# Zero-tile matmuls in PE's planned waits: two layers of memory attention and gated FFN

## The chip, the core and the metric

The kernel runs on one core of one Trainium2 chip. The metric is the device time of one execution in microseconds (us), as the median of several runs. Engines are named as in the profile: PE is TensorE (PEld its weight loads), DVE VectorE, ACT ScalarE, POOL GpSimd, SP SyncE, which here only issues DMAs.

## The reference

Inputs are bf16. `A` is attention over segments of 32 tokens with 8 memory tokens carried from one segment to the next; `B` is a gated feed-forward. The same weights are used twice.

```python
# x: 1 x 2048 x 512; 32 heads of 128; memory 8, segment 32; F = 1792
def A(x, mem0):                       # x is layer-normed
    mem = mem0
    for s in range(64):
        h = concat([mem, x[:, 32*s:32*s+32]])            # 40 tokens
        q, k, v = h @ Wq, h @ Wk, h @ Wv                 # 32 heads
        p = softmax(where(mask, q @ k.T * scale, -1e9))
        o = (p @ v) @ Wo                                 # summed over heads
        mem = o[:, :8]; outs.append(o[:, 8:])
    return concat(outs)
def B(x): return (sigmoid(x @ w_gate) * (x @ w_up)) @ w_down

x = x + A(layernorm(x)); x = x + B(layernorm(x))
x = x + A(layernorm(x)); x = x + B(layernorm(x))
```

## The kernel before

The 64 segments must follow one another, since each takes its memory from the one before. The second layer's attention starts 6 steps behind the first (`lag=6`), so there are 70 steps; in steps 6 to 63 both layers' segments are worked on together (`both`, 80 columns), and at the beginning and the end one alone (40 columns). `emit_step` writes one step: for groups of six heads, the q and k projections (L734, 40 or 80 columns streamed past 128x128 weights), their eviction by ACT into `qku`, the scores (L748), mask, max, exp, sum and product on DVE and ACT (L762 to L780) into `pb`, a transpose on PE (L791) and its copies into `ptsb`, the product with v (L814), an eviction into `otsb`, and the output projection (L832), which accumulates all heads into one bank `WB`. The memory columns of `WB` are copied into the next step's `hT` by DVE (L845, L850). The v rows of the memory come from `strips` (L660, four 32-row outputs beside each other), those of the tokens from `v_pass` (L583, 512 columns), which go to a DRAM scratch `scr` and are read back into `vsb` by DMA (L703). `layernorm_T` transposes a normalised block of 128 tokens (L552); `ffn` runs a block of 128 tokens through the gated feed-forward (L900 transposes, L932 gate and up, L956 down), with weights streamed by POOL.

At the beginning, in the boot, SP issues all attention weights in pieces (L484), and `v_group` runs `v_pass` for many blocks whose results are staged in the FFN's weight tiles and stored to `scr`.

The order of work is not written by hand. Each piece is a `Task` with an engine, a planned duration and its reads and writes. `Planner.plan` runs a list scheduler over all tasks with these planned times, 24 rounds, and keeps the shortest; it also assigns buffers, among them the eight PSUM banks (`bank`). `run` then emits the tasks in the order of their planned starts, and each engine keeps that order. Semaphore waits are put in from the tiles that are read and written. The planned start of a task, `tk.start`, and the planned duration, `tk.dur`, are still there when the instructions are emitted. A matmul of n columns is planned with `max(n / 2.4 + 2.3, 26.0)` ns.

Of the kernel before, what the change touches and what calls it, by code (L numbers as in the profile page):

```python
# [2 lines left out]

# [6 lines left out]
BF16 = mybir.dt.bfloat16  # L10
# [6 lines left out]
P = 128  # L17
# [14 lines left out]
def mm_ns(n):  # L32
    return max(n / 2.4 + 2.3, 26.0)
# [13 lines left out]


class Task:
    __slots__ = ("eng", "dur", "lat", "fn", "deps", "succ", "tail", "boost", "ndep", "ready", "start", "idx", "on", "fresh", "acq", "rel", "durs", "tick", "prev", "land", "adj", "banks")  # L50

    def __init__(self, eng, dur, lat, fn, boost):
        self.durs = dur if isinstance(dur, dict) else {e: dur for e in eng}
        self.eng, self.dur, self.lat, self.fn, self.boost = eng, min(self.durs.values()), lat, fn, boost
        self.deps, self.succ, self.fresh = set(), [], set()
        self.acq, self.rel = [], []
        self.on = None
        self.land = 3000.0
        self.adj = {}
        self.banks = ()  # L60


class Buf:

    __slots__ = ("pool", "kind", "users", "first", "left", "slot", "t_free", "t_prev", "rd")
# [16 lines left out]
class Planner:  # L82
# [3 lines left out]
    LAT = {"PE": 205.0, "DVE": 110.0, "ACT": 128.0, "POOL": 40.0, "SP": 4000.0}  # L86
    TO_PE = 32.0
    WAIT = 65.0

    def __init__(self):  # L90
        self.tasks = []
        self.writer = {}
        self.readers = {}
        self.bufs = []
# [6 lines left out]
    def add(self, eng, dur, fn, r=(), w=(), lat=None, boost=0.0, use=(), late=0.0):  # L101
        engs = eng if isinstance(eng, tuple) else (eng,)
        tk = Task(engs, dur, self.LAT[engs[0]] if lat is None else lat, fn, boost)
        tk.idx = len(self.tasks)
        for k in r:
            if k in self.writer:
                tk.deps.add(self.writer[k])
                tk.fresh.add(self.writer[k])
        for k in w:
            if k in self.writer:  # L110
                tk.deps.add(self.writer[k])
            for q in self.readers.get(k, ()):
                tk.deps.add(q)
        for k in w:
            self.writer[k] = tk.idx
            self.readers[k] = []
        for k in r:
            self.readers.setdefault(k, []).append(tk.idx)
        tk.deps.discard(tk.idx)
        if late:  # L120
            tk.adj = {d: late for d in tk.fresh if self.tasks[d].eng == ("PE",)}
        self.tasks.append(tk)
        if engs[0] != "PE":
            tk.banks = tuple(k for k in r if isinstance(k, Buf) and k.pool.psum)
        for k in list(r) + list(w) + list(use):
            if isinstance(k, Buf) and (not k.users or k.users[-1] != tk.idx):
                k.users.append(tk.idx)
        return tk
# [78 lines left out]
    def forward(self):  # L207
# [126 lines left out]
        order.sort(key=lambda k: (k.start, k.idx))  # L334
        return order

    def waits(self, tk, seen):

        T = self.tasks
        need = {}  # L340
        for d in [T[i] for i in list(tk.deps) + tk.prev]:
            k = d.on if d.on != "SP" else ("SP", d.tick)
            if d.tick > seen.get(k, 0):
                need[k] = max(need.get(k, 0), d.tick)
        seen.update(need)
        return len(need)
# [10 lines left out]
class Kern:  # L357
# [40 lines left out]
    def setup_tiles(self):  # L398
        ctx, tc, nc = self.ctx, self.tc, self.nc
        D, DC, H, HG, F, FC, R = self.D, self.DC, self.H, self.HG, self.F, self.FC, self.R  # L400
        HE = H * P
        c = ctx.enter_context(tc.tile_pool(name="c", bufs=1))
        dr = ctx.enter_context(tc.tile_pool(name="dr", bufs=1, space=bass.MemoryType.DRAM))
        self.scr = [dr.tile([self.NSEG * XS, HE], BF16, name=f"scr{j}") for j in range(2)]
        self.wq = c.tile([P, DC, HE], BF16, name="wq_sb")
        self.wk = c.tile([P, DC, HE], BF16, name="wk_sb")
        self.wv = c.tile([P, DC, HE], BF16, name="wv_sb")
        self.wo = c.tile([P, H, D], BF16, name="wo_sb")
        cst = c.tile([P, P + 2 * L + 8], BF16, name="cst")
        self.ident, self.maskb, self.mask1 = cst[:, 0:P], cst[:, P:P + L], cst[0:L, P + L:P + 2 * L]  # L410
        self.negh = cst[:, P + 2 * L:P + 2 * L + 2].bitcast(F32)
        small = c.tile([P, 48], F32, name="small")
        self.lns = [small[:, 10 * i:10 * i + 10] for i in range(3)]
        self.mx = [small[:, 30 + 6 * i:36 + 6 * i] for i in range(3)]
        self.NV = 3
        self.hT = [c.tile([P, DC, 2 * L], BF16, name=f"hT{i}") for i in range(R)]
        self.qku = [c.tile([P, 3, 2, LW], BF16, name=f"qku{i}") for i in range(3)]
        self.vsb = [c.tile([P, 2, 1024], BF16, name=f"vsb{i}") for i in range(self.NV)]
        self.st = [c.tile([P, HG, L], F32, name=f"st{i}") for i in range(3)]
        self.pb = [c.tile([LW, HG, 64], BF16, name=f"pb{i}") for i in range(3)]  # L420
        self.ptsb = [c.tile([P, HG, 2, L], BF16, name=f"ptsb{i}") for i in range(3)]
        self.otsb = [c.tile([P, HG, 2 * L], BF16, name=f"otsb{i}") for i in range(2)]
        self.NX = 6
        self.xs = [c.tile([P, D], BF16, name=f"xs{i}") for i in range(self.NX)]
        self.xa = [c.tile([P, D], BF16, name=f"xa{i}") for i in range(2)]
        self.oxT = [[c.tile([P, DC, P], BF16, name=f"oxT{j}_{i}") for i in range(2)] for j in range(2)]
        self.xn = [c.tile([P, D], BF16, name=f"xn{i}") for i in range(2)]
        self.xnT = [c.tile([P, DC, P], BF16, name=f"xnT{i}") for i in range(1)]
        self.hff = [c.tile([P, FC, P], BF16, name=f"hff{i}") for i in range(1)]
        self.th = [c.tile([P, 2, P], F32, name=f"th{i}") for i in range(2)]  # L430
        self.xvf = [c.tile([P, DC, P], BF16, name=f"xvf{i}") for i in range(2)]
        self.xvl = [c.tile([P, DC, P], BF16, name=f"xvl{i}") for i in range(3)]
        self.vst = [c.tile([P, 512], BF16, name=f"vst{i}") for i in range(3)]
        self.sst = [c.tile([P, 2, 512], BF16, name=f"sst{i}") for i in range(1)]
        self.NG, self.ND = 3, 3
        self.wg = [c.tile([P, DC, 2 * P], BF16, name=f"wg{i}") for i in range(self.NG)]
        self.wu = [c.tile([P, DC, 2 * P], BF16, name=f"wu{i}") for i in range(self.NG)]
        self.wd = [c.tile([P, 2, D], BF16, name=f"wd{i}") for i in range(self.ND)]
        pp = ctx.enter_context(tc.tile_pool(name="ps", bufs=1, space=PSUM))
        self.bank = Pool([pp.tile([P, 512], F32, name=f"bank{i}") for i in range(8)], {"bg": 3, "v": 3}, psum=True)  # L440
        self.qkp = Pool(self.qku)
        self.vstp = Pool(self.vst)
        self.sstp = Pool(self.sst)
        self.bootp = Pool([fview(w[:, 0, 0:1], [(1, 1024)]) for w in self.wd + self.wg + self.wu])
        self.xnp = Pool(self.xn)

    def setup_consts(self):
        nc, tc = self.nc, self.tc
        cmasks.make_identity(nc, self.ident[:])
        NEG = -1.0e9 / self.scale  # L450
        nc.gpsimd.memset(self.maskb[:], 0.0)
        nc.gpsimd.memset(self.mask1[:], 0.0)
        nc.gpsimd.affine_select(out=self.mask1[:], in_=self.mask1[:], pattern=[[-1, L]],
                                compare_op=ALU.is_ge, fill=NEG, base=0, channel_multiplier=1)
        nc.gpsimd.memset(self.mask1[0:MEM, :], 0.0)
        nc.gpsimd.affine_select(out=self.maskb[0:L, 0:SEG], in_=self.maskb[0:L, 0:SEG], pattern=[[-1, SEG]],
                                compare_op=ALU.is_ge, fill=NEG, base=0, channel_multiplier=1)
        nc.vector.memset(self.negh[:], -0.5)

    def clear(self):  # L460
# [208 lines left out]
    def emit_step(self, t):  # L669
# [10 lines left out]
        nj = len(jobs)  # L680
        full = slice(0, LW)
        hkeys = [("hT", slot, j, k) for j in jobs for k in ("m", "x")]

        c0 = 0 if both else L * j0

# [166 lines left out]
        for idx, j in enumerate(jobs):  # L852
# [3 lines left out]
            dst = self.oxT[j][oi][:, :, (s % BLK) * SEG:(s % BLK + 1) * SEG]  # L856
            pl.add("ACT", 160, lambda dst=dst, a=48 * j - c0: (dst, wo3(a, SEG)), r=[WB], w=[("oxT", j, oi, s % BLK)])

    def last_weights(self):

        if self.lw is None:
# [163 lines left out]
    def run(self):  # L1025
# [3 lines left out]
        order = self.pl.plan()  # L1029
        with self.tc.manual_schedule():  # L1030
            self.setup_consts()
            for tk in order:
                got = tk.fn()
                if isinstance(got, tuple) and len(got) == 3:
                    {"SP": nc.sync, "POOL": nc.gpsimd}[tk.on].dma_start(out=got[1], in_=got[2])
# [63 lines left out]
```

## Time and profile before

| | |
|---|---|
| median of 9 runs | 1827.17 us (1823.74 to 1830.45) |
| the profiled execution | 1825.57 us |
| its span, first to last instruction | 1823.8 us |
| mean granted PE clock over the span | 0.995 |
| PE busy | 1761.5 us, 97% |
| DVE, ACT, POOL busy | 1177.6, 1175.6, 580.2 us |
| longest groups | L734 622.4 and 621.4 us, L832 367.1 us, L932 172.2 and 171.6 us |
| DMA | 271.18 MB, mean 149 GB/s; 341 GB/s in the first of 40 slices |
| PE's longest sums of waits | otsb from ACT before L832 9.1 us (31 times), xn from DVE before L552 7.6 us (5 times) |

A line of a group or of the timeline gives the start, the busy time, engine, line, operation, tiles written and read, the shape and the number of instructions, and in brackets the engine's idle time just before with what ended it. A row of the table of windows gives the stretch, its length, busy time and number of instructions of each engine, the granted PE clock (1.00 is full), the share of the DMA engines' time and the GB/s moved. Matmul records overlap, because matmuls are pipelined: the distance of the starts is the time that one takes.

### The profile page before, as it was taken

How to read it: one execution, taken by the hardware profiler on the slowest of the kernel's cores; microseconds unless marked ns; L12 is line 12 of the kernel's file. 1: busy time of each engine (PE TensorE's matmuls, PEld its weight loads, DVE VectorE, ACT ScalarE, POOL GpSimd, SP SyncE). 2: the span in 40 equal slices, each digit the busy share in tenths (PEclk: the TensorE clock that was granted, in tenths of full speed). 3: DMA queues.
4: the chain of work that ended last, by engine and by line, in shares of the span. 5: the costliest groups of instructions: out<-in, count | busy, mean ns of one | idle time of the engine just before them, and what ended most of it. 6: DMA issues, size and time to landing. Idle time of an engine off the chain costs nothing.

```text
span 1823.8 us, 91963 instructions
## 1 busy us (share of the span) xinstructions
PE 1761.5 (97%) x39743; PEld 1521.7 (83%) x39942; DVE 1177.6 (65%) x3933; ACT 1175.6 (64%) x2969; POOL 580.2 (32%) x838
## 2 busy tenths in 40 slices
PE   7999999999999999999999999999999999999998
PEld 3677787988888898988888898888888898889886
DVE  4466565676676567666666667666766676566665
ACT  5666666676666666665666666666666666566664
POOL 7223031413333242423324142323324231332422
PEclk9999999999999999999999999999999999999999
DMA  9734252636555464645446463555546453554543
GB/s 341 242 108 141 55 149 82 196 104 176 143 153 162 115 182 113 173 126 171 144 129 188 112 184 108 153 151 149 163 115 189 128 158 107 167 147 117 174 126 109
DMA packets 137096, 271.18 MB, mean 149 GB/s; under 512 B 32698, under 2 KB 69186, under 8 KB 136690
## 3 DMA queue, kind: packets, MB, share of 16 engines
q0 software_dynamic: 56736, 183.35, 34.1%
q1 hardware_dynamic: 79954, 81.94, 15.7%
q8 instruction: 313, 5.13, 1.2%
q14 instruction: 93, 0.76, 0.1%
HBM read 220.93 MB, written 26.21 MB: 136 GB/s over the span
## 4 chain that ended last, share of the span: by engine, by line
PE 86%; ACT 5%; SPq 3%; DVE 3%; issue 2%; DMA 1%; POOL 0%; ACTq 0%; POOLq 0%; DVEq 0%
PE bank L734 32%; PE bank L832 17%; PE bank L932 9%; PE bank L660 7%; PE bank L583 6%; PE bank L956 4%; PE bank L748 4%; PE bank L814 3%; SPq L484 3%; PE bank L791 2%; ACT qku L1039 1%; ACT ptsb L1039 1%; ACT otsb L1039 1%; PE bank L552 1%; DVE st L762 1%
## 5 line engine op out<-in xcount | busy, mean ns | idle before, releaser
L734 PE MATMUL bank<-hT,wq_sb 128*128 128x80 bf16 (+1 forms) x8960 | 622.4, 198 | 8.7 <-issue 4.6
L734 PE MATMUL bank<-hT,wk_sb 128*128 128x80 bf16 (+1 forms) x8960 | 621.4, 198 | 2.8 <-DMA wk_sb<-in_A_Wk_dram 2.7
L1039 ACT CAST qku<-bank 128x480 bf16<-128x480 f32 (+3 forms) x770 | 391.4, 512 | 253.8 <-PE bank L734 184.4
L734 PEld LDWEIGHTS <-wq_sb 128*128 128x128 bf16 x8960 | 454.7, 99 | 38.3 <-issue 27.5
L734 PEld LDWEIGHTS <-wk_sb 128*128 128x128 bf16 x8960 | 450.4, 99 | 4.2 <-DMA wk_sb<-in_A_Wk_dram 3.2
L762 DVE TENSOR_TENSOR st<-bank,cst 40x240 f32<-40x240 f32 (+3 forms) x768 | 279.1, 367 | 227.0 <-PE bank L748 219.4
L832 PE MATMUL bank<-otsb,wo_sb 128*128 128x80 bf16 (+1 forms) x8960 | 367.1, 198 | 10.8 <-ACT otsb L1039 9.1
L924 POOL DMA_DIRECT2D wg<-in_B_w_gate_dram x217 | 164.8, 760 | 647.5 <-PE bank L932 623.7
L832 PEld LDWEIGHTS <-wo_sb 128*128 128x128 bf16 x8960 | 342.0, 99 | 24.0 <-issue 15.1
L1039 ACT CAST otsb<-bank 128x480 bf16<-128x480 f32 (+3 forms) x420 | 196.3, 486 | 72.5 <-PE bank L814 53.7
L950 POOL DMA_DIRECT2D wd<-in_B_w_down_dram x217 | 153.5, 710 | 154.7 <-PE bank L791 71.9
L1039 ACT COPY ptsb<-bank 40x240 bf16<-40x240 bf16 (+2 forms) x552 | 173.9, 316 | 38.7 <-PE bank L791 30.4
L772 ACT ACTIVATE st<-st 80x240 f32<-80x240 f32 (+3 forms) x420 | 159.4, 382 | 37.0 <-DVE st L769 32.8
L774 DVE TENSOR_REDUCE small<-st 80x6 f32<-80x240 f32 (+3 forms) x420 | 151.7, 364 | 47.0 <-ACT st L772 44.1
L932 PE MATMUL bank<-xnT,wg 128*128 128x128 bf16 (+2 forms) x1784 | 172.2, 219 | 1.1 <-ACT xnT L1039 0.5
L932 PE MATMUL bank<-xnT,wu 128*128 128x128 bf16 (+2 forms) x1784 | 171.6, 219 | 0.0
L925 POOL DMA_DIRECT2D wu<-in_B_w_up_dram x217 | 162.8, 750 | 3.2 <-issue 2.5
L769 DVE TENSOR_TENSOR st<-st,small 80x240 f32<-80x240 f32 (+3 forms) x420 | 154.0, 369 | 4.0
L767 DVE TENSOR_REDUCE small<-st 80x6 f32<-80x240 f32 (+3 forms) x420 | 152.6, 365 | 5.5
L779 DVE TENSOR_TENSOR pb<-st,small 80x240 bf16<-80x240 f32 (+3 forms) x420 | 152.5, 369 | 4.5
L748 PE MATMUL bank<-qku 128*128 128x80 bf16 (+1 forms) x2240 | 154.1, 198 | 1.1 <-ACT qku L1039 0.2
L542 POOL TENSOR_TENSOR small<-small,cst 128x1 f32<-128x1 f32 (+1 forms) x80 | 44.5, 557 | 346.4 <-DVE small L541 343.9
(93 smaller groups left out, 2248.7 us busy)
## 6 DMA issues: line engine op xcount, KB each, us to landing
wg<-in_B_w_gate_dram POOLq DMA_DIRECT2D x220, 256.0 KB, 4.1
wu<-in_B_w_up_dram POOLq DMA_DIRECT2D x220, 256.0 KB, 4.7
wd<-in_B_w_down_dram POOLq DMA_DIRECT2D x220, 256.0 KB, 4.8
vsb<-scr SPq DMA_DIRECT2D x476, 48.0 KB
vsb<-sst SPq DMA_DIRECT2D x480, 32.0 KB
scr<-vst SPq DMA_DIRECT2D x120, 96.0 KB
wq_sb<-in_A_Wq_dram SPq DMA_DIRECT2D x10, 384.0 KB
wk_sb<-in_A_Wk_dram SPq DMA_DIRECT2D x10, 384.0 KB
```

The costliest lines, as they stand in the source:

```text
L734: nc.tensor.matmul(o_ap, lhsT=W[:, c, h * P:(h + 1) * P], rhs=mv(c), start=(c == 0), stop=(c == DC - 1))
L748: nc.tensor.matmul(s_all(SB)[:, w0 + i, :], lhsT=fview(qku[:, i, 0, 0:1], [(1, P)]), rhs=qku[:, i, 1, 0:ncol], start=True, stop=True)
L762: pl.add("DVE", dve_ns(n, True), lambda gsz=gsz, hs=hs, st=st, SB=SB, pj_=pj_, npj_=npj_, mk=mk, idx=idx: nc.vector.tensor_tensor(out=st[p ...
L767: pl.add("DVE", dve_ns(n), lambda hs=hs, st=st, mx=mx: nc.vector.tensor_reduce(out=mx[pr, hs], in_=st[pr, hs], axis=AX.X, op=ALU.max), r=s ...
L769: pl.add("DVE", dve_ns(n), lambda gsz=gsz, hs=hs, st=st, mx=mx: nc.vector.tensor_tensor(out=st[pr, hs], in0=st[pr, hs], in1=mx[pr, hs].uns ...
L772: pl.add("ACT", act_ns(n), lambda hs=hs, st=st: nc.scalar.activation(out=st[pr, hs], in_=st[pr, hs], func=ACTF.Exp, scale=self.scale), r=s ...
L832: nc.tensor.matmul(WB[:, c * ncol:(c + 1) * ncol], lhsT=self.wo[:, h, c * P:(c + 1) * P], rhs=otsb[:, hl, 0:ncol], start=(h == 0 and c == ...
L924: pl.add("POOL", 760, lambda wg=wg, fs=fs: nc.gpsimd.dma_start(out=wg[:], in_=self.wgv[:, :, fs]), r=[("wo", self.H - 1)], w=[gk] + bt, la ...
L925: pl.add("POOL", 760, lambda wu=wu, fs=fs: nc.gpsimd.dma_start(out=wu[:], in_=self.wuv[:, :, fs]), r=[("wo", self.H - 1)], w=[uk] + bt, la ...
L932: nc.tensor.matmul(gu[:, 2 * i + k, 0:n], lhsT=W[:, c, i * P:(i + 1) * P], rhs=xnT[:, c, rw], start=(c == 0), stop=(c == DC - 1))
L950: pl.add("POOL", 760, lambda wd=wd, ip=ip: nc.gpsimd.dma_start(out=wd[:], in_=self.wdv[:, 2 * ip:2 * ip + 2, :]), w=[dk] + (["boot"] if se ...
L1039: nc.scalar.copy(out=dst, in_=src)
```

## The change

A 128x128 bf16 tile `hot` is set to zero by DVE at the start. Each task carries a `rate`: the share of its planned time in which PE is taken to stream, 0.95 in general and `ncol / 2.4 / mm_ns(ncol)` in an attention step (0.64 for 40 columns, 0.94 for 80). After planning, `warm` goes through PE's tasks in planned order. Where a task is the first user of a PSUM bank and its planned start lies more than 250 ns after the planned end of what precedes it on PE (at the beginning after 1.2 us), and the task is planned in the first 8 us or one of eleven windows of 3.413 us around the gap holds less than 60% planned streaming, it notes a number of 128-column units: the planned gap less 120 ns, at 1.2 columns per ns in the first 8 us, at 2.4 after. `run` emits these ahead of the task as matmuls with `hot` as weights and as moving operand, up to four units (512 columns) each, into the bank that the task acquires; the task's own first matmul overwrites it.

```diff
     LAT = {"PE": 205.0, "DVE": 110.0, "ACT": 128.0, "POOL": 40.0, "SP": 4000.0}
     TO_PE = 32.0
     WAIT = 65.0
+    SPAN, COLD, WARM0 = 3413.0, 8000.0, 1200.0
...
+    def warm(self, order):
+
+        pe = [tk for tk in order if tk.on == "PE"]
+        at, run = [tk.start for tk in pe], [0.0]
+        for tk in pe:
+            run.append(run[-1] + tk.dur * tk.rate)
+
+        def done(t):
+            i = bisect.bisect_right(at, t)
+            return run[i - 1] + min(pe[i - 1].dur, t - at[i - 1]) * pe[i - 1].rate if i else 0.0
+
+        fill, end = {}, self.WARM0
+        for tk in pe:
+            gap, on = tk.start - end, [bf for bf in tk.acq if bf.pool.psum]
+            if gap > 250.0 and on:
+                cold = tk.start < self.COLD
+                lo = min(done(x + self.SPAN) - done(x) for x in (end - self.SPAN + gap + k * 0.1 * (self.SPAN - gap) for k in range(11))) if gap < self.SPAN else 0.0
+                if cold or lo < 0.6 * self.SPAN:
+                    n = int((gap - 120.0) * (1.2 if cold else 2.4)) // P
+                    if n > 0:
+                        fill[tk.idx] = (on[0], n)
+            end = max(end, tk.start + tk.dur)
+        return fill
...
+        self.hot = c.tile([P, P], BF16, name="hot")
...
+        nc.vector.memset(self.hot[:], 0.0)
         nc.vector.memset(self.negh[:], -0.5)
...
         order = self.pl.plan()
         with self.tc.manual_schedule():
             self.setup_consts()
+            fill = self.pl.warm(order)
             for tk in order:
+                if tk.idx in fill:
+                    B, n = fill[tk.idx]
+                    while n > 0:
+                        m = min(n, 4)
+                        nc.tensor.matmul(B[:, 0:m * P], lhsT=self.hot[:], rhs=fview(self.hot[:, 0:1], [(0, m), (1, P)]), start=True, stop=True)
+                        n -= m
                 got = tk.fn()
```

## The prediction

> **What bounds the kernel now.** I read the page first, then the table of windows, the timeline and the chain of waits. The page:
>
> ```profile
> span 1823.8 us, 91963 instructions
> PE 1761.5 (97%) x39743; PEld 1521.7 (83%) x39942; DVE 1177.6 (65%) x3933; ACT 1175.6 (64%) x2969; POOL 580.2 (32%) x838
> PEclk9999999999999999999999999999999999999999
> ```
>
> PE is busy for 97% of the span, so time is won only where PE works slower than it could. In slices of 46 us the clock looks full everywhere, but the mean granted clock is 0.995: some stretches run at half rate. A table of short windows finds them:
>
> ```profile
> core 0: us, PE busy (x) PEld busy (x) DVE busy (x) ACT busy (x) POOL busy (x), PEclk, DMA share, GB/s
> 61.53:64.94 3.41, 1.84 (x32) 1.15 (x31) 0.00 (x0) 1.27 (x3) 2.17 (x4) 1.00 1.09 371
> 126.38:129.80 3.42, 0.76 (x15) 0.51 (x12) 1.67 (x6) 1.88 (x8) 0.00 (x0) 1.00 1.00 272
> 129.80:133.21 3.41, 2.79 (x60) 2.50 (x60) 2.93 (x12) 2.75 (x11) 0.00 (x0) 0.50 0.09 30
> 133.21:136.62 3.41, 3.38 (x78) 3.17 (x76) 1.97 (x11) 1.77 (x8) 0.55 (x1) 0.50 0.11 34
> 174.17:177.58 3.41, 1.85 (x62) 1.67 (x59) 0.74 (x4) 1.00 (x5) 2.36 (x4) 1.00 0.89 270
> 177.58:181.00 3.42, 3.05 (x35) 1.24 (x32) 0.55 (x3) 1.52 (x5) 0.00 (x0) 0.50 0.38 127
> 1720.41:1723.82 3.41, 1.60 (x45) 1.39 (x42) 3.15 (x12) 3.15 (x14) 0.00 (x0) 1.00 0.09 22
> 1723.82:1727.24 3.42, 3.12 (x83) 3.12 (x82) 2.44 (x11) 2.11 (x10) 0.00 (x0) 0.50 0.02 5
> 1795.50:1798.92 3.42, 1.60 (x43) 1.33 (x40) 2.00 (x8) 1.64 (x7) 2.32 (x4) 1.00 1.03 310
> 1798.92:1802.33 3.41, 3.41 (x74) 3.41 (x72) 2.60 (x11) 2.12 (x7) 0.08 (x1) 0.50 0.91 274
> ```
>
> Next to last is the clock. Five windows at 0.50 while PE had work, 17.1 us: four follow a window in which PE had little, one follows another slow one. All lie on one grid of 3.413 us. The timeline prices them and shows the beginning; the last line is a piece of the chain of waits:
>
> ```profile
> 10.98 3.24 PE L583 MATMUL bank<-wv_sb,xvf 128*128 128x512 bf16 x8 [0.62 <-DVE xvf L1041]
> 15.40 0.40 PE L552 MATMUL bank<-cst,xn 128*128 128x128 bf16 x4 [0.96 <-DVE xn L543]
> 24.71 1.89 PE L583 MATMUL bank<-wv_sb,xvf 128*128 128x512 bf16 x8
> 64.59 0.27 PE L734 MATMUL bank<-hT,wk_sb 128*128 128x40 bf16 x4 [1.57 <-DMA wk_sb<-in_A_Wk_dram]
> 138.22 1.91 PE L660 MATMUL bank<-wv_sb,hT 128*32 128x512 bf16 x32
> 178.02 3.36 PE L660 MATMUL bank<-wv_sb,hT 128*32 128x512 bf16 x32 [0.37 <-DVE hT L850]
> ...
> 64.72 5.49 DMA wk_sb<-in_A_Wk_dram
> ```
>
> Eight 512-column matmuls take 3.24 us at 10.98 and 1.89 us at 24.71: about 0.40 and 0.22 us each, so the start is at half rate too, though no clock record covers it. The chain of the first 70 us is the issue and landing of weight loads (SP L484 65.5% of it, then this wk_sb landing).
>
> **What moves the clock.** I count columns by the matmul records. A 512-column matmul starts every 0.215 us, 0.42 ns a column, so a 3.413 us window holds some 8,190 at full rate. Before a drop: 800 columns at 126.38 (10%), 2,672 at 174.17 (33%), 2,472 at 1720.41 (31%), 2,168 at 1795.50 (26%). At 61.53, with the matmul running into it, 43%, and the clock stayed. So the limit for a drop lies between 33% and 43%. Upwards, of half-rate capacity: the window at 129.80 streamed 67% and stayed slow; the one from 10.33 had 81% and ended it. The busy column above doesn't separate these (1.84 us kept the clock, 1.85 lost it), since each matmul's record has a tail.
>
> **The change by its parts.** It adds 81 matmuls on `hot` with 35,840 columns at 27 places, a DVE memset, and no other instruction; every other engine keeps its order. The matmuls go into the bank that the next task owns; in the instruction order three fills wait for an evicting engine, where the next real matmul would have. Fills in a real wait cost nothing; a fill where no wait comes is paid.
>
> *Gains after the boot (bounds: 0 to the row's value).*
> - 177.58: a fill of 768 columns lands in the 1.56 us wait for xn at 177.05, and the front of another. 33% becomes 44%, just above what kept the clock. L660's 32 matmuls then take 1.84 to 1.91 us instead of 3.36: 1.5 us, and PE is full after it. Taken whole.
> - 1723.82: 2,944 columns in the 1.15 us wait at 1722.66 and 1,024 in the 0.96 us wait at 1724.12 make 31% into 79%. L832's 72 matmuls are 33 ns apart there, 25 in warm rows: 0.6 us; four groups of three 80-column matmuls 0.06 each. 0.84, of which 0.7, as some ends in ACT waits.
> - 133.21: the window before it stays slow (10% and two small fills make 23%), but there 768 columns at half rate make 67% into 86%, so the second slow window goes. Its extra streaming, counted the same way, is 0.9; taken 0.6.
> - 1798.92: one fill of 384 columns makes 26% into 31%. It stays: the 1.66 us wait at 1797.44 is within a matmul group, where no fill stands. 0.
>
> Sum 2.8 us, between 0 and 3.3.
>
> *Paid fills.* At 197.60 L814 follows L791 without a wait and gets 1,664 columns before it, 0.69 us. ACT, which copies otsb out at 198.73, is busy with its exp until 198.83, and L791 at 199.06 waits for DVE's pb in any case: 0.2 (0 to 0.69). At 1781.88 640 columns, 0.27 us, come before an L791 with no wait; a 0.36 us wait for otsb follows: 0 (to 0.27). At 116.90 0.69 us stand in a distance of 0.76: 0. The rest are shorter than their waits: 0.2 in all for drift of waits. Cost 0.4.
>
> *The beginning.* Fills of 3,072 and 2,560 columns lie in the waits before 3.96 and 7.67 (3.96 and 3.45 us): free. The window 6.92 to 10.33 still streams 23% to 27%, so PE is slow at 10.98 as before. Then 1,152 columns come between two L583 groups that have no gap (2.25 x 0.40 = 0.9 us), and 7,936 (15.5 x 0.215 = 3.3 us) before the transposes at 15.40, whose wait is 0.96. PE's path: 10.98 + 1.6 + 0.9 + 1.0 + 0.3 + 3.3 = 18.1 instead of 15.4, 2.7 us late. L583 evictions and the POOL's stores to scr queue behind that. PE's waits for weight DMA at 55.47, 64.59, 68.98, 69.78 and 70.25 (0.62, 1.57, 0.24, 0.53, 0.20) sum to 3.16 us and take it up; the weights come by SP, which waits for nothing on PE. Cost 0 (-0.3 to 2.7; below nothing, as later stores leave the loads more of the DMA). So too, warming earlier there would gain nothing.
>
> Sum: -2.8 + 0.4 = **-2.4 us**. The profiled execution took 1825.57 (span 1823.8 and 1.8 around it); it would become 1823.2. It is 1.60 below the median of nine, 1827.17. The grid's place under the kernel is not the kernel's: laying it at 40 places under the recorded matmuls, with limits of 38% and 75%, gives 5.0 slow windows after 50 us on average (the profiled placing has five) and 2.5 with the fills, and streaming lost of 7.1 and 3.2 us at most. That bounds the gain by 3.9. I take the profiled placing's 2.4: 1827.17 - 2.4 = **1824.8**.
>
> The Trainium skill, "TensorE: Matmul & The Clock Gate", section "HAM oscillation — how this bites in real kernels", speaks against the change: it asks only that PE have no idle gaps over about 3.4 us. After the beginning no wait here reaches that (the longest is 2.40 us), yet the clock fell four times; so the measured windows decide. By that rule the fills would save 0 and the sum would be +0.4.
>
> **The rivals.**
> - *No window is lifted* (0.20): an all-zero tile, or 44%, may not count as enough. For it: only one window, 43%, shows the upper side of the limit. Against: the records order all cases by streaming. Time: 1827.17 + 0.4 = 1827.6.
> - *The grid pays fully* (0.27): the median execution has longer slow chains than the profiled one. At some placings 1783 to 1800 gives six slow windows in a row, and none with the fills. For it: the median's 1.60 us above the profile. Against: some lost streaming hides in ACT and DVE waits. 3.9 or more: 1823.2, down to 1821.
> - *Slower: the boot's fill is on the path* (0.08). If work after 70 us hangs on PE's v_pass (L583, evictions, scr) rather than the weights, the 7,936 columns are paid. At full rate that is 2.7 us, which the gains nearly cancel; at half rate 15.5 x 0.40 + 0.9 - 1.0 = 6.1 us, less 2.4: +3.7, 1830.9. It decides from a lateness over 3.16 us on. Against: every PE wait from 55 to 70 us names a weight DMA.
>
> **How the numbers follow.** 0.2% of 1827.17 is 3.65 us, about what a measurement of this kernel can tell from no change. My forecast (0.45) and the first rival fall inside; of the second nearly all is outside, and the third half. Faster than 1823.5: 0.29; within: 0.65; slower than 1830.8: 0.06. Where PE waits inside one matmul group for no shown reason (five waits before L734, 4.6 us) the added instructions may move them by a microsecond. Range: from below the second rival's time, 1821.0, to the boot paid at full rate without the 177.58 gain, 1827.17 - 2.4 + 2.7 + 1.5, rounded to 1829.0.
>
> **What would show it.** L1072 in the lines, near 81 matmuls; transposes at about 18 us instead of 15.4; PE's wait for wk_sb near 64 us shrunk, and wk_sb landing near 70 us as before; L660 near 178 us in 1.9 us; clock 1.00 in the window after 1723.8; a slow window still near 130 and near 1799, if the grid lies alike. Wrong if windows with fills at 44% or more still lose the clock, if the first wk matmul after 70 us is late, or if L832 near 199 is over 0.5 us late against its step.

## The result: 0.3% faster, and the profile after

| | before | after |
|---|---|---|
| median | 1825.7 us (55 runs, 1821.43 to 1833.07) | 1820.74 us (18 runs, 1818.38 to 1823.55) |
| ratio, 95% interval | | 0.997 [0.9963, 0.9977], that is -5.5 us (the medians differ by 5.0) |
| the profiled execution, span | 1825.57, 1823.8 us | 1820.98, 1819.2 us |

The change is faster, by more than the forecast's 2.4 us, and the median lies 0.26 us below the range. The zero fills are L1072; lines of the kernel before are 31 to 34 higher now (L734 is L766, L660 L691, L583 L614, L552 L583, L748 L780, L791 L823, L814 L846, L832 L864). From the page after:

```profile
span 1819.2 us, 92125 instructions
...
PE 1774.2 (98%) x39823; PEld 1524.9 (84%) x40023; DVE 1178.3 (65%) x3934; ACT 1179.2 (65%) x2969; POOL 581.6 (32%) x838
...
q8 instruction: 314, 5.14, 1.2%
```

PE has 81 more weight loads, 80 more matmuls in the records, and one more DVE instruction; the other engines do what they did. PE is busier and the span is shorter. The last line, the queue that brings instructions, will matter below. The windows after that answer to those of before:

```profile
core 0: us, PE busy (x) PEld busy (x) DVE busy (x) ACT busy (x) POOL busy (x), PEclk, DMA share, GB/s
129.46:132.88 3.42, 3.39 (x62) 2.55 (x59) 3.12 (x14) 2.61 (x10) 0.00 (x0) 0.50 0.08 23
132.88:136.29 3.41, 3.17 (x87) 2.60 (x85) 1.80 (x11) 1.63 (x7) 0.55 (x1) 1.00 0.10 31
173.84:177.25 3.41, 2.15 (x39) 1.12 (x38) 0.90 (x4) 1.22 (x5) 1.25 (x2) 1.00 0.88 282
177.25:180.66 3.41, 3.41 (x87) 2.70 (x80) 0.06 (x1) 2.04 (x4) 0.00 (x0) 1.00 0.15 46
1716.66:1720.08 3.42, 2.88 (x49) 1.75 (x48) 3.11 (x14) 3.17 (x14) 0.00 (x0) 1.00 0.00 0
1720.08:1723.49 3.41, 3.41 (x92) 2.38 (x90) 1.27 (x6) 2.34 (x7) 0.00 (x0) 1.00 0.02 5
1788.34:1791.75 3.41, 2.13 (x78) 2.03 (x78) 1.84 (x8) 0.99 (x3) 2.92 (x5) 1.00 1.04 308
1791.75:1795.17 3.42, 3.35 (x56) 2.99 (x53) 3.34 (x13) 2.81 (x10) 1.27 (x2) 0.50 1.04 301
```

Of the five windows at 0.50 the three that were to go are gone: the second of the pair at 130, the one at 177 and the one at 1720. The two that were to stay, near 130 and near 1792, stayed. The columns say that the fills did it: the windows from 173.84 and 1716.66 streamed 0.50 and 0.66 of what a window holds at full rate, and would hold 0.31 and 0.25 without the fills; in none of the 18 traces of this case did a window with 0.35 or less keep the clock (between 50 and 1805 us, the strip matmuls counted once for the four that run beside each other).

One profile is one placing of the grid, though. In time it lies 0.3 us from that of before, but the work has moved by 1.1 to 5.8 us, so the windows cut it elsewhere, and in a second trace of before (below) neither 178 nor 1724 is slow, without any fill. What speaks for more than one execution is the granted clock of every run: 0.9967 in the mean of after's 18 runs, 0.9951 in 126 runs of before that were taken beside the kernels below.

The timeline of PE after, at the places that the prediction named:

```profile
14.52 3.51 PE L1072 MATMUL bank<-hot 128*128 128x512 bf16 x16
17.86 0.39 PE L583 MATMUL bank<-cst,xn 128*128 128x128 bf16 x4
...
176.58 1.91 PE L691 MATMUL bank<-wv_sb,hT 128*32 128x512 bf16 x32
...
194.61 0.87 PE L1072 MATMUL bank<-hot 128*128 128x512 bf16 x4
195.32 0.60 PE L846 MATMUL bank<-ptsb,vsb 104*128 104x80 bf16 x12
```

The transposes of the boot start at 17.86 instead of 15.40, the 32 strip matmuls take 1.91 us instead of 3.36. I matched every matmul of before with its own in after and took the difference of the starts. It is +2.46 us at 15.40, +1.68 at 55.5, -0.05 at 64.6 (the weight waits have taken it up), -1.1 from 73 on, -1.6 at 135 (window at 133 gone), -2.9 at 199 (window at 177 gone) and stays near there until 320. At 328 it falls back to -2.0, where PE in after waits 0.80 us for `vsb` (L846). Then come steps where no fill stands and the clock is full in both: -3.0 from 629, -4.2 from 1148, -5.6 from 1564. At 1720 a wait that before doesn't have (0.60 us, for issue) makes it -5.0, and the lifted window there brings it back to -5.7. The steps at 629, 1148 and 1564 are not in the prediction. At the first of them before has this, in PE's timeline:

```profile
628.41 0.20 PE L734 MATMUL bank<-hT,wq_sb 128*128 128x80 bf16 x1
629.45 0.27 PE L734 MATMUL bank<-hT,wq_sb 128*128 128x80 bf16 x3 [0.84 <-issue]
```

One group of four matmuls breaks after its first, and PE waits 0.84 us for nothing that the profile names. After has no such wait there. The waits of PE between 400 and 1700 us (engine and line, what ended them, us in total, times, longest), first before, then before once more, then after:

```profile
PE bank L734 <- issue: 2.9, 4, 1.2
```

```profile
PE bank L734 <- issue: 5.2, 6, 1.4
PE bank L660 <- issue: 1.5, 1, 1.5
...
```

```profile
PE bank L614 <- issue: 0.3, 2, 0.2
```

So two causes are in play: slow windows lifted, and waits inside matmul groups that vanished from this stretch. Not from the whole kernel: after 1700 us after still has such waits of 0.60, 1.42 and 1.15 us, at 1715, 1790 and 1796. The experiments take the two causes apart.

### The profile page after: what moved, and what is told of

It is laid out like the page before. It is cut to its first block, busy times and chain, and to the rows that moved or that the text cites. A ratio compares the mean times of both kernels' runs of the same rounds, so it can differ in the third digit from the quotient of the medians.

```text
span 1819.2 us, 92125 instructions
## 1 busy us (share of the span) xinstructions
PE 1774.2 (98%) x39823; PEld 1524.9 (84%) x40023; DVE 1178.3 (65%) x3934; ACT 1179.2 (65%) x2969; POOL 581.6 (32%) x838
## 4 chain that ended last, share of the span: by engine, by line
PE 88%; ACT 5%; DVE 3%; issue 2%; POOL 1%; SPq 0%; DMA 0%; POOLq 0%; ACTq 0%; DVEq 0%
PE bank L766 32%; PE bank L864 17%; PE bank L966 9%; PE bank L614 8%; PE bank L691 7%; PE bank L990 4%; PE bank L780 4%; PE bank L846 3%; PE bank L823 2%; ACT qku L1080 1%; ACT ptsb L1080 1%; ACT otsb L1080 1%; PE bank L583 1%; DVE st L794 1%; ACT st L804 1%
## 5 line engine op out<-in xcount | busy, mean ns | idle before, releaser
L766 PE MATMUL bank<-hT,wq_sb 128*128 128x80 bf16 (+1 forms) x8960 | 621.5, 198 | 3.2 <-DVE hT L877 2.4
L766 PE MATMUL bank<-hT,wk_sb 128*128 128x80 bf16 (+1 forms) x8960 | 621.2, 198 | 1.4 <-issue 1.4
L766 PEld LDWEIGHTS <-wq_sb 128*128 128x128 bf16 x8960 | 454.6, 99 | 33.2 <-issue 22.8
L766 PEld LDWEIGHTS <-wk_sb 128*128 128x128 bf16 x8960 | 450.5, 99 | 1.5 <-issue 1.5
L864 PE MATMUL bank<-otsb,wo_sb 128*128 128x80 bf16 (+1 forms) x8960 | 365.1, 198 | 10.0 <-ACT otsb L1080 8.8
L864 PEld LDWEIGHTS <-wo_sb 128*128 128x128 bf16 x8960 | 340.1, 99 | 23.9 <-issue 14.6
L780 PE MATMUL bank<-qku 128*128 128x80 bf16 (+1 forms) x2240 | 154.4, 198 | 1.7 <-issue 0.6
```

The lines of the kernel that those rows point to most:

```text
L766: nc.tensor.matmul(o_ap, lhsT=W[:, c, h * P:(h + 1) * P], rhs=mv(c), start=(c == 0), stop=(c == DC - 1))
L780: nc.tensor.matmul(s_all(SB)[:, w0 + i, :], lhsT=fview(qku[:, i, 0, 0:1], [(1, P)]), rhs=qku[:, i, 1, 0:ncol], start=True, stop=True)
L864: nc.tensor.matmul(WB[:, c * ncol:(c + 1) * ncol], lhsT=self.wo[:, h, c * P:(c + 1) * P], rhs=otsb[:, hl, 0:ncol], start=(h == 0 and c == ...
```

## The experiments

Results are ratios to before, run beside them on the same chip, with 95% intervals. Where one is turned into us, 1825.7 us is taken as 1.

### Which places pay

**Before, run again**, to see what another profiled execution of it shows.

> The kernel before, once more, for a second profile. Theory A (slow windows and the boot make the difference): the four places of slow windows, 130, 178, 1724 and 1799, show again where the grid lies alike; waits inside one q/k matmul group (4.56 us in the first profile, 1.42 after the change) may differ by a microsecond or two, since they are chance. Theory B (the added instructions moved those waits): they stand again at 629, 1148, 1564 and 1797 us with about 4.6 us in all.

Measured: 1828.77 us, span 1827.0, clock 0.997, as high as after's. It is 3.2 us longer than the first profile, though 10.2 us of it are at half rate after the boot (128.09 to 134.92 and 1807.45 to 1810.86) and 17.1 of the first. Its lines are the second of the three fences above: 6.7 us of waits inside groups in a stretch where the first profile has 2.9. One trace had shown me less than half of that term.

**The same instructions, nothing streamed.** Every fill becomes a matmul of 8 columns.

```diff
- nc.tensor.matmul(B[:, 0:m * P], lhsT=self.hot[:], rhs=fview(self.hot[:, 0:1], [(0, m), (1, P)]), start=True, stop=True)
+ nc.tensor.matmul(B[:, 0:8], lhsT=self.hot[:], rhs=self.hot[:, 0:8], start=True, stop=True)
```

> Every fill matmul is kept but streams 8 columns instead of up to 512: the same instructions in the same places, next to no streaming. Theory A: the slow windows near 130 to 137, 178 and 1724 come back, and with them 2 to 3 us; the boot is no longer late, so its 1.1 us goes too; time within 0.1% of the kernel before (1824 to 1827). Theory B: the waits inside q/k groups stay as small as after the change, and some 3 us of the gain are kept (1822 to 1823).

Measured: 1.0002 [0.9993, 1.0011]. Without columns there is no gain at all, which speaks for the clock alone. I repeated it later:

> The kernel with all fills cut to 8 columns, once more. It has 62 instruction pairs ahead of its middle like the runs with a shifted stream, which were 0.16% faster, but measured 1.0002 of the kernel before (0.9993 to 1.0011), with more slow windows (mean clock 0.9940 against 0.9953). If that was the chance of eleven placings of the grid: 2 to 3 us faster than before now, clock near 0.995. If small matmuls in the waits themselves cost time or clock: again no difference, clock near 0.994.

Measured: 1.0004 [0.9995, 1.0012]. The two agree; I come back to them at the end, because they fit the rest badly.

**Fills after 20 us only, fills of the boot only, the 14 places between 20 and 400 us, the 8 places after 400 us.** Each is one line after `warm`:

```diff
+ fill = {k: v for k, v in fill.items() if self.pl.tasks[k].start > 20000.0}             # late
+ fill = {k: v for k, v in fill.items() if self.pl.tasks[k].start < 20000.0}             # boot
+ fill = {k: v for k, v in fill.items() if 20000.0 < self.pl.tasks[k].start < 400000.0}  # mid
+ fill = {k: v for k, v in fill.items() if self.pl.tasks[k].start > 400000.0}            # end
```

> Only the fills after the boot (22 of the 27 places). Theory A: windows lifted as after the change, gain 2.5 to 3.5 us; transposes back at 15.4 us, weight loads landing at 70.2 us again, so some 1 us slower than the changed kernel. If the late PE in the boot cost time in most executions, this one is instead faster than the changed kernel by 1 to 2 us.

> Only the five fills of the boot. Theory A: PE 2.5 us late at 15.4 us, on time again at 65 us, and ahead by about 1.1 us after 70 us because the last weights land earlier; the slow windows at 130, 178, 1724 stay; gain 0.5 to 1.5 us. If the 1.1 us were chance, no difference to the kernel before. Theory B: 25 added instruction pairs ahead of everything shift what follows as in the changed kernel, gain about 3 us.

> Only the 14 places between 116 and 307 us of the first profile. Theory A (gain = slow windows lifted, as an average over the grid's placings): counted by streamed columns with the limits that all six traces show (lost below 40%, regained above 72%), the placings lose 4.2 us here on average before and 1.5 with the fills: gain 2.5 to 3, time near 1823.2. Theory C (the profiled placing is typical): the windows at 133 and 178 alone, 1.5 to 2.1 us.

> Only the 8 places from 1721 us on. Theory A: lost streaming of the placings there is 2.3 to 4.3 us on average without fills and 0.9 to 2.5 with them: gain 1.4 to 2, time near 1824.2; together with the run before it makes the whole gain. Theory C: the window at 1724 alone, 0.7 us.

| fills | matmuls ahead of 400 us | ratio |
|---|---|---|
| late | 31 | 0.9973 [0.9964, 0.9982] |
| boot | 31 | 0.9993 [0.9984, 1.0002] |
| mid | 31 | 0.9966 [0.9953, 0.9978] |
| end | 0 | 0.9997 [0.9987, 1.0007] |

The whole gain comes with the mid fills alone, some 12,700 columns at 14 places; the boot's fills can be left out, and those of the end bring nothing that can be measured. The boot's interval (-0.4 to 2.9 us) takes in both of its forecasts and decides nothing. The mid fills' gain, 6.2 us (4.0 to 8.6), is above both of theirs and more than the mid windows are worth (1.5 + 0.6 by the sum), so the rest comes through something that mid fills do besides holding the clock. The waits of 400 to 1700 us are fewer in their trace, but not gone (1.8 us, three times).

**Larger fill before 130 us, and without the two paid fills** (at 197.60 and 1781.88). 30 units (3,840 columns) are put where the window before 130 is thin.

```diff
+ fill = {k: v for k, v in fill.items() if self.pl.tasks[k].start > 20000.0 and k not in (1309, 13014)}
+ fill[780] = (fill[780][0], 30)
```

> The late fills without the two that stood in no wait (197.60 and 1781.88), and with 3,840 columns instead of 640 in the 2.0 to 3.0 us wait before L814 at 129 us; no boot fills. Theory A: the slow stretch near 130 goes for all placings, 1 to 1.5 us more gain, time 1819.3 to 1820. If the wait there is not idle in most executions, the fill delays L814 and the gain is that of the late fills alone or less (1821 or more).

Measured: 0.9969 [0.9956, 0.9981], not to be told from after or from the late fills. The 1 to 1.5 us that were hoped for did not come: in the profile PE is still at half rate from 131.46 to 138.28. The paid fills cost nothing that shows, but the two edits were not run apart.

**A longer boot fill**, 124 units instead of 62 before the transposes, to see how much lateness the weight loads cover.

```diff
+ fill[136] = (fill[136][0], 124)
```

> The changed kernel with the boot's last fill doubled (15,872 instead of 7,936 columns before the transposes at 15.4 us). PE comes 5.8 us late to them instead of 2.5. If the waits for weights up to 70 us are a cover of 3.2 us, as the prediction had it, 2.6 us are left over: 1823 to 1824. If the cover is larger because later stores let the weights land earlier or later, the result lies elsewhere: no change means a cover of 6 us, plus 3.3 us means none is left after 2.5.

Measured: 0.9974 [0.9964, 0.9985]. That is 4.7 us, 0.7 less than after's 5.5, with intervals that overlap; the profile says more. The fill and the transposes behind it, from its timeline:

```profile
15.73 6.98 PE L1073 MATMUL bank<-hot 128*128 128x512 bf16 x31
22.55 0.39 PE L583 MATMUL bank<-cst,xn 128*128 128x128 bf16 x4
```

The transposes are 7.15 us late against before. PE's waits for weights between 30 and 75 us, in before and in the kernel with late fills only:

```profile
PE bank L734 <- DMA wk_sb<-in_A_Wk_dram: 2.7, 3, 1.6
...
```

```profile
PE bank L766 <- DMA wk_sb<-in_A_Wk_dram: 2.3, 3, 1.0
```

With the long fill no wait for a weight load is left there (nor is one in after), and a matmul that runs at 75.02 us in before and at 73.94 in after runs at 78.25. Of 7.15 us of lateness 3.2 go through, so the waits for weights covered 3.9 us; the prediction had counted 3.16. Traces with no 512-column fills in the boot lie between -0.8 and +1.6 us at this point, so the two figures agree, and after's 1.1 us can't be put down to its fills.

### Columns against place in the instruction stream

In before, in before repeated and in the kernel with the end fills, the unexplained waits between 400 and 1700 us fall on one set of places, counted in PE's instructions (weight loads and matmuls) without the fills: 21,614, 26,204, 35,388, 39,978, 49,160, 51,456, 58,344, 62,934 and 67,526. No execution has them all, and what one lasts differs from one to the next. The instruction queue moved 313 packets of 5.13 MB / 313 = 16.4 KB; 313 x 256 is 80,128, and before has 79,685 PE instructions in its records (39,942 weight loads and 39,743 matmuls; with a matmul for each load it would be 79,884). That suggests that PE reads its instructions in packets of 256 and waits where a packet comes late. If so, moving the stream by less than a packet changes where the border falls, and moving it by a whole one does not.

**Before, with zero matmuls of 8 columns ahead of all other work**: 62 (124 instructions, as many as after has by 400 us), 128 (256, one packet), and 31.

```diff
+ B = next(bf for tk in order if tk.on == "PE" for bf in tk.acq if bf.pool.psum)
+ for _ in range(62):        # 128, 31
+     nc.tensor.matmul(B[:, 0:8], lhsT=self.hot[:], rhs=self.hot[:, 0:8], start=True, stop=True)
```

> The kernel before with 62 zero matmuls of 8 columns (124 PE instructions) ahead of PE's first work, none in any wait: as many PE instructions as the changed kernel has ahead of its middle. Theory A+B (two parts: slow windows lifted, some 3 us; and the shifted instruction stream, some 2.5 us, by fewer waits inside tasks): 2 to 3 us faster than before, waits inside tasks between 400 and 1700 us down from 3 to 7 us to below 1.5, slow windows as before. Theory A alone: no difference.

> The same with 128 such matmuls, 256 instructions: at 64 B an instruction PE's stream moves by 16.4 KB, which is one packet of the instruction queue (5.13 MB in 313 packets). Theory A+B with the place in the packet as the cause: the waits inside tasks are back at 3 to 7 us and the time is that of the kernel before within 1 us. If any added instruction helps, 2 to 3 us faster as with 62. Theory A alone: no difference.

> The same with 31 (62 instructions), as many as the boot fills alone add. Theory A+B: 1.5 to 3 us faster, as the boot fills alone were (1823.9 against 1826.0 in the mean), waits inside tasks from 400 to 1700 us below 1.5. Theory A alone, or the boot's later PE as the cause there: no difference.

**After, with 66 of them ahead**, so that from 400 us on its stream too stands one whole packet later: the fills stay, the shift is undone.

```diff
+ B = next(bf for tk in order if tk.on == "PE" for bf in tk.acq if bf.pool.psum)
+ for _ in range(66):
+     nc.tensor.matmul(B[:, 0:8], lhsT=self.hot[:], rhs=self.hot[:, 0:8], start=True, stop=True)
```

> The changed kernel with 66 more matmuls of 8 columns ahead of all work: with the 62 fills before its middle these are 128, a whole packet. Theory A+B: the slow windows stay lifted but the waits inside tasks return, so 2 to 3 us are lost: a gain of about 3 us on the kernel before instead of 5.5. Theory A alone: all of the 5.5 us stay.

| kernel | instructions ahead | ratio | waits inside groups, 400 to 1700 us | mean clock of 12 runs (before beside them: 0.9949) |
|---|---|---|---|---|
| before + 31 | 62 | 0.9984 [0.9976, 0.9993] | 0 | 0.9959 |
| before + 62 | 124 | 0.9984 [0.9974, 0.9995] | 0 | 0.9952 |
| before + 128 | 256 | 1.0003 [0.9992, 1.0013] | 5.1 us | 0.9952 |
| after + 66 | 256 | 0.9986 [0.9975, 0.9996] | 2.8 us | 0.9971 |

(The column of waits leaves out the `v_pass` lines, 0.3 to 0.5 us in all of these kernels, as in before.) The lines of the second and the third kernel, then of after + 66, from PE's waits between 400 and 1700 us:

```profile
PE bank L585 <- issue: 0.3, 2, 0.2
```

```profile
PE bank L736 <- issue: 5.1, 5, 1.6
...
```

```profile
PE bank L766 <- issue: 2.2, 4, 0.8
PE bank L691 <- issue: 0.6, 1, 0.6
...
```

Zero matmuls of 8 columns, put where no work is yet, make before 2.9 us faster (0.0016 x 1825.7; the interval gives 0.9 to 4.7), and with 62 of them the clock is that of before. A whole packet of them brings the waits back and the gain goes: in before + 128 they stand at 35,644, 40,234, 49,416, 58,600 and 67,782, each exactly 256 after a place named above. After with the shift undone keeps 2.6 us (0.7 to 4.6), with a higher clock; four of its waits stand at 26,460, 49,416, 63,190 and 67,782, again 256 after places of before (a fifth, of 0.18 us, at 28,756). Shift and fills together make 2.9 + 2.6 = 5.5 us, what the change brought, closer than their intervals of some 2 us either way let one claim.

The traces settle what these waits are. Counted over the whole stream, fills included, every wait for issue outside `v_pass` after 400 us, in all 18 traces, lies on one comb with teeth 256 apart, to within 2 instructions (the slow slide of the comb taken out); one at 79,006 is in 14 of the traces, whether 0 or 160 instructions were added ahead of it. And the DMA records hold each packet of the instruction queue, 16,384 bytes: all 90 waits for issue outside `v_pass` from 135 us on end 1.2 to 1.8 us after such a packet has landed (the wait that ends at 629.45 in before: landed at 628.19). At the other packet borders the landing is 3.9 us back in the median. So PE waits for a late packet. Late means that its transfer starts late: that packet starts 3.8 us after the border before it, against 0.6 us in the median, and takes 1.2 us, near the usual 1.1. At 626 to 629 us of before the DMA engines are at 0.94 to 0.97 of their time with weights of the feed-forward; that the packets queue behind them is argued, not shown.

### What is left open

**Tiny fills at the mid places, and in the boot, alone**, to see why the tiny fills at all places were not faster although they shift the stream too.

> Only the 14 places from 116 to 307 us, each fill matmul with 8 columns: the stream is shifted by 31 pairs from there on, and small matmuls stand in those waits. If small matmuls in waits cost time or clock, no faster than before with a clock near 0.994. If it is the boot's small matmuls that undo the gain, 2 to 3 us faster as with a shifted stream alone.

> Only the five places of the boot with 8 columns each, 31 matmuls: the same shift as with 31 ahead of all work (which was 0.16% faster), but spread over the first 18 us. If the boot's small matmuls are harmless: 2 to 3 us faster than before, as there. If they undo the gain: no difference.

Measured: mid 0.9988 [0.9977, 0.9998], boot 0.9994 [0.9985, 1.0003]. The mid ones have the gain of a shift; the boot's interval takes in its smaller forecast and none at all. In all these kernels the waits of 400 to 1700 us are nearly gone (0 and 0.2 us; 1.0 and 0.2 with tiny fills everywhere), so tiny fills everywhere should have gained too and did not. Their clock is lower, in the two profiles (0.992 and 0.993 against 0.995 before) and over all their runs (0.9940 and 0.9937; before beside them 0.9953 and 0.9951). What that costs can be read from the runs: over 302 of them, each taken against the mean of its kernel and round, 0.001 less clock goes with 1.0 us more (0.84 to 1.16). With that taken out, tiny fills everywhere are 1.6 and 1.2 us faster than before. The twelve kernels that shift the stream by part of a packet are 2.2 us faster in the mean (0.0 to 4.1), and the three that don't, or shift it by a whole one (end fills, before + 128, after + 66), lie between 0.6 us faster and 0.9 slower. So the shift does gain there, and the clock takes it back; why it is lower there was not tried.

**The larger fill with a shift**: the kernel with 3,840 columns before 130 us, and 31 matmuls ahead.

> Late fills without the two unneeded ones, 3,840 columns in the wait before L814 near 129 us, no boot fills, and 31 matmuls of 8 columns ahead of all work, so that the stream is shifted by about as much as in the changed kernel (the run without them had 1.2 us of waits inside tasks near 131 us). Theory A+B: slow time 6 to 7 us instead of 12, at a third of a microsecond each 1 to 2 us faster than the changed kernel: 1818.8 to 1820. If the shift does not matter there: 1821 to 1822 as without it.

Measured: 0.998 [0.9971, 0.9989], 1822.01 us. Its clock is the best of all, 0.998 in the profile and 0.9989 over its runs, and it is no faster than after; the 1818.8 to 1820 that were hoped for did not come. By the slope above its clock alone accounts for the 3.9 us that it gains in the mean, and of the shift nothing is seen, though the waits of 400 to 1700 us are gone: that stays open. No version here beats the change as it is; the one with late fills only, 1820.82 us, equals it.

## Why the prediction was right or wrong

- **The bound, the windows, the term for them: right.** The three windows that the column count named are gone, and the two that it left are there. In the matched starts the lifted windows are worth 1.5 us at 178, 0.8 at 1724 and 0.6 at 133, where 1.5, 0.7 and 0.6 were booked. The 2.8 - 0.4 = 2.4 us of the sum stand against 2.6 us (0.7 to 4.6) in the run that undoes the shift. That two of these windows are full in a second trace of before shows that the profiled placing was not every placing, so the agreement is partly luck; the end fills alone gave 0.9997, where 0.7 us was booked. Two small figures of the working are off, and nothing rests on them: the upper bounds of the gains add up to 3.24 us, not 3.3, and 2,472 columns are 30% of 8,190, not 31%.
- **The rule on idle gaps.** The Trainium skill, "TensorE: Matmul & The Clock Gate", section "HAM oscillation — how this bites in real kernels", would make the fills useless here, since no wait after the beginning is over 3.4 us. After + 66 lies at 0.9986, and its interval leaves out both 1 and the +0.4 us that the rule gave. The same page's next section, "A second HAM failure mode: psum-queue depth-cycling", says of another kernel that short idle times between groups of matmuls, when they are frequent enough, make the clock swing too; that agrees with the four windows of before that lost the clock with waits of at most 2.40 us.
- **Paid fills: small, as said or smaller.** L846 starts at 195.32, 0.6 us late against its step; at 199 nothing is left of it, and the kernel without both paid fills, which also had the larger fill, can't be told from the one with them (0.9969).
- **The boot: right.** 2.46 us late at the transposes (2.7 forecast), gone at 64.6 us where PE waited for wk_sb. The longer fill puts the end of the cover at 3 to 4 us, so "slower: the boot's fill is on the path" fell for the reason given. Nor did warming the start gain: leaving these fills out made no difference.
- **The step that failed** is the sentence on the waits "inside one matmul group for no shown reason (five waits before L734, 4.6 us) the added instructions may move them by a microsecond". It stood in the sum at 0 and entered neither end of the range. It measured 2.9 us (0.9 to 4.7), as large as all of the rest. I had taken a wait without a named cause as noise of that execution, and its size from one trace; a second trace of before shows 6.7 us where the first shows 2.9. I had also looked for effects only where fills stand. An added instruction moves every later one against the packet borders, and these waits are PE waiting for a late packet at a border.
- **The base.** The forecast started from the median of nine runs, 1827.17; that of 55 is 1825.7. Of the 4.06 us between 1824.8 and 1820.74 these 1.47 are the base, and the other 2.6 are gain that the sum did not have. Counted from its own base the range allowed a gain of 6.2 us, so the measured 5.0 to 5.5 lie inside it as a gain, though at twice what was forecast; the median fell below the range only because the base was high as well.
- **The rivals.** "No window is lifted" fell with the windows and the higher clock of after's runs. "The grid pays fully" had nearly the right time, 1823.2 down to 1821, for another reason: it needed 3.9 us or more from the clock. The runs with the shift undone give no sign of that much (2.6), though the interval does not exclude it.

## What to carry to other kernels

A wait that the profile puts down to nothing but issue is a term of the sum: look whether it comes back at the same instruction count in a second execution, and if so try the kernel with some dozens of idle instructions ahead of everything, before crediting a change that adds instructions with what it was made for. A change that adds instructions is itself tested with as many more ahead as make a whole packet, so that its own effect stands alone. Don't take one profile's slow windows for all: compare the granted clock of all runs. Price a slow window from the rows of its own place, and count what streams in the window before it, not the length of the waits.

## What the runs showed of the hardware

- Between 400 and 1700 us PE stops for 0.2 to 1.6 us inside groups of matmuls, at borders of the 256-instruction packets of its instruction queue, and goes on 1.2 to 1.8 us after the packet has landed. The places repeat from run to run and move by exactly 256 when 256 instructions are put ahead. Counted modulo 256 they slide evenly, from 92 at 26,204 to 158 - 256 = -98 at 79,006: 190 in 52,800, or 0.4%, as if that share of the stream were not in the trace (313 x 256 is 0.3% more than two instructions for each recorded weight load).
- The clock, by the columns streamed per window of 3.413 us, in all 18 traces (strip matmuls and the last 20 us as above): at full rate every window with up to 0.35 of what it can hold lost the clock and every one from 0.41 on kept it; between them both occur (0.356 kept, 0.402 lost). At half rate, counted against half-rate capacity, every window under 0.69 was followed by another slow one and none over 0.86 was; between them both occur (0.698 regained, 0.853 not). Counted so, the window at 129.80 that the prediction has at 67% comes to 0.70. Matmuls on an all-zero tile count like others: without them the window at 173.84 of after would hold 0.31, with them it holds 0.50, and the clock held.
- The beginning can be warmed, and it doesn't last: after's clock came up at 6.59 us and fell again at 10.0; the window between streamed 0.125.
